# Moving the inverse of block 2 behind the weight conversion, and block 2's solve five steps later in block 1

## The chip, the cores and the metric

The kernel runs on one core of one Trainium2 chip. The metric is device time in microseconds (us). PE is the matmul engine, PEld its weight loads, DVE the vector engine, ACT the scalar engine, SP the engine whose queue issues most DMAs.

## The reference

A delta-rule attention for 4 sequences of 8 heads, 768 time steps of width 48, followed by a two-layer network:

```python
k_n = k / (np.linalg.norm(k, axis=-1, keepdims=True) + 1e-06)
for t in range(S):                       # state: one 48 x 48 matrix per head
    y[:, :, t] = q_t @ state
    state = state + beta_t * outer(k_t, v_t - state^T k_t)
x = y.transpose(0, 2, 1, 3).reshape(B * S, H * D)    # 3072 x 384
h = x @ w_in                                          # 384 x 2048
out = np.maximum(0.01 * h, h) @ w_out                 # 2048 x 384
```

All in float32; each network matmul is done as three matmuls over split operands (a high part and a remainder).

## The kernel before

The 768 steps are cut into 12 blocks of 64. For block n there are these pieces, each a Python generator that is advanced one step at a time:

- `gram(n)`: two steps (groups). It loads k and q, forms the products of the keys with keys and queries on PE (`pg`, L201), copies them (L205), masks the query part on DVE (`rq`, L216; `gm`, L220), and sends the key part through DRAM (`gd`) into the tile `L`.
- `inv(b)`: 33 steps, blocks 0 and 1 together as b = 0, then block n as b = n - 1, so block 2 is b = 1. It clears the tile `T` (L280), calls `norms` (twelve short DVE instructions, L239 to L248), scales `L` (L289, L292), and then makes 31 elimination steps, each of up to two products (`tmp`, L263) and two subtractions (L268) on DVE. At the end ACT makes a transposed copy (L299) and SP writes both to DRAM (`td`, `tt`; L307, L308). `T` has one buffer, so the next inverse's clearing waits until those transfers have read it.
- `solve(n)`: five steps. It loads the inverse back (`rt`, `gm`; L318, L320) and goes through matmuls and copies `pz`, `zs`, `pu`, `rt`, `pk`, `pw`, `pc`, `py`, `ys`. It needs the inverse of block n and the state of block n - 1. A DVE step in it, `rv` (L388), scales keys and values by the norms.
- `ffn(n)`: the network on the 256 rows of block n, in 16 steps over f; step f makes nine matmuls `ph` (L468), two ACT instructions (`gh`, L472, L473), one DVE remainder (`gl`, L475), and six matmuls `po` (L458) two steps later; `gh` and `gl` have three buffers each. A seventeenth step first calls `columns(n + 1)`, which turns `ys` of the next block into the split operands `xh`, `xl` (`px` L443, L115, L116), and then writes the output. `ffn(n + 1)` can't start without those.
- `weights()`: 32 chunks, each some seven DVE instructions (L148 to L161) and two ACT ones, which unpack the network's weights from 64-bit words. Four are converted early, 28 run into block 0. `ffn(0)` step f needs chunks 2f and 2f + 1.

The function `weave(n_slots, (generator, steps, a, b), ...)` traces one step of each slot in turn and spreads `steps` of a generator evenly over the slots a to b. In block n there are 17 slots: `ffn(n)` in all, the weights in 0 to 12 of block 0, `solve(n + 1)` in 2 to 11, `inv` (of block n + 2) in 2 to 17, `gram` in 11 to 13. A generator that needs another (`need`) advances it first.

The order of the trace is only a priority. The framework puts the instructions in order per engine by a simulated timeline: of those that are ready, the one traced first goes. On the chip each engine then works through its list in that fixed order. `behind(name)` adds an order on one engine: what it encloses is put behind a marked instruction. In `norms`, the first DVE instruction is put behind the last `gl` traced so far.

Of the kernel before, what the change touches and what calls it, by code (L numbers as in the profile page):

```python
# [14 lines left out]
ALU = mybir.AluOpType  # L15
# [10 lines left out]
NGR = NSEQ // GS  # L26
# [21 lines left out]
def delta_moe_kernel(ctx: ExitStack, tc, kqT, kv, qT, beta, cst, w_all, out, nblk):  # L48
# [10 lines left out]
    nc = tc.nc  # L59
    NFC, _, DO = w_all.shape[1:]  # L60
# [47 lines left out]
    raws, mark = {}, {}  # L108

    def behind(name):  # L110

        return tc.issue_after(mark[name]) if name in mark else nullcontext()
# [5 lines left out]
    def load_w(k, gate=None):  # L118
        if k < 2 * NFC:
            raws[k] = raw = sb.tile([P, DO], U64, tag=f"w{k}", name=f"wr{k}", bufs=1)  # L120
            if gate:
                with behind(gate):
                    nc.vector.memset(raw[:, 0:1].bitcast(F32), 0.0)
            with behind("L"):
                nc.sync.dma_start(raw, w_all[:, k // 2, k % 2])

    def weights():

        for k in range(2 * NFC):
            f, x = k // 2, k % 2
            words = raws.pop(k).bitcast(F32).rearrange("p (n two) -> p two n", two=2)
            lo, hi = words[:, 0], words[:, 1]
            loi, hii = lo.bitcast(U32), hi.bitcast(U32)
            g = sb.tile([P, DO], F32, tag="cg", name=f"cg{k}", bufs=CB)
            r = sb.tile([P, DO], F32, tag="cr", name=f"cr{k}", bufs=1)
            gi, ri = g.bitcast(U32), r.bitcast(U32)

            def final():  # L140
                t = sb.tile([P, 2 * DO], F32R, tag=f"w{k}", name=f"w{k}", bufs=1)
                for e in range(2):
                    (wi, wo)[x][e][f] = t[:, e * DO:(e + 1) * DO]
                return (w[f] for w in (wi, wo)[x])

            nc.scalar.activation(g, hi, AF.Abs)
            with behind("inverse" if k >= KA else None):
                i = nc.vector.tensor_scalar(g, g, HI_MIN, HI_MAX, ALU.max, ALU.min)  # L148
            mark["work"] = i.ins
            if k + WAHEAD >= WEARLY:  # L150
                load_w(k + WAHEAD, "work")

            e = sb.tile([P, DO], F32, tag="ce", name=f"ce{k}", bufs=1)
            nc.vector.tensor_scalar(gi, gi, 3, 0x3FFFF000, ALU.logical_shift_left, ALU.bitwise_and)
            nc.vector.scalar_tensor_tensor(gi, hii, 0xC0000000, gi, ALU.bitwise_and, ALU.bitwise_or)  # L155
            nc.vector.tensor_scalar(ri, hii, 0x1FF, 14, ALU.bitwise_and, ALU.logical_shift_left)
            nc.vector.scalar_tensor_tensor(ri, loi, 18, ri, ALU.logical_shift_right, ALU.bitwise_or)  # L157
            nc.vector.tensor_scalar(e.bitcast(U32), gi, 0xFF800000, None, ALU.bitwise_and)
            d0, d1 = final()
            nc.scalar.copy(d0, g)  # L160
            nc.vector.scalar_tensor_tensor(d1, ri, 2.0 ** -34, e, ALU.mult, ALU.mult)  # L161
            yield

    Lh, gm, nrm, Tts, ys, xs, done = {}, {}, {}, {}, {}, {}, set()
# [5 lines left out]
    def dq(n):  # L170

        return nc.scalar if n < 2 else nc.sync
# [58 lines left out]
    def norms(n, n2):  # L231

        p, w = P, HC
        s, r, c, z = (sb.tile([P, wd], F32, tag=t, name=f"{t}{n}", bufs=b)
                      for t, wd, b in (("sr", HC, 1), ("rc", HC, 1), ("cb", HC, 2), ("sq", C, 2)))
        nrm[n] = z
        dq(2 * n).dma_start(c, beta[n])
        with behind("gl"):
            nc.vector.tensor_scalar(s.bitcast(U32), n2.bitcast(U32), 1, None, ALU.logical_shift_right)  # L239
        nc.vector.tensor_scalar(s, s, SQRT_SCALE, 1e-30, ALU.mult, ALU.max)  # L240
        for f in (NEWTON, 0.5):
            nc.vector.reciprocal(r, s)
            nc.vector.scalar_tensor_tensor(r, r, f, n2, ALU.mult, ALU.mult)
            nc.vector.scalar_tensor_tensor(s, s, f, r, ALU.mult, ALU.add)
        nc.vector.tensor_scalar_add(s, s, EPS)
        nc.vector.reciprocal(r, s)
        nc.vector.tensor_tensor(c, c, r, ALU.mult)
        nc.vector.tensor_tensor(c, c, r, ALU.mult)  # L248
        for e in range(2):
            nc.scalar.mul(z[:, e * HC:(e + 1) * HC], s, half[:, e:e + 1])  # L250
        return c
# [20 lines left out]
    def inv(b):  # L272
# [8 lines left out]
        yield  # L281
        L = Lh.pop(b)
        c = norms(b, L.rearrange("p m i -> p (m i)")[:, ::HC + 1])
        if two:
            nc.vector.tensor_copy(X[:, ::HC + 1], c)
# [208 lines left out]
    def chain(fn, blocks):  # L494
        for n in blocks:
            yield from fn(n)

    def weave(n_slots, *streams):

        taken = [0] * len(streams)  # L500
        for i in range(n_slots):
            for k, (gen, steps, a, b) in enumerate(streams):
                want = steps if i >= b - 1 else max(0, i + 1 - a) * steps // (b - a)
                while taken[k] < want:
                    next(gen, None)
                    taken[k] += 1

    NS, NF, NI = NSLOT, NFC + 1, HC + 1
    wg = weights()
    gg = chain(gram, range(nblk))  # L510
    iv = chain(inv, range(len(NB)))
    sv = chain(solve, range(nblk))
    ff = chain(ffn, range(nblk))
# [10 lines left out]
        load_w(k)  # L524
    for n in range(nblk):

        weave(NF, (ff, NF, 0, NF), (wg, 2 * NFC * (n == 0), 0, 12), (sv, NS * (n + 1 < nblk), 2, 11),
              (iv, NI * (n + 2 < nblk), 2, NF), (gg, NGR * (n + 3 < nblk), 11, 13))


WAHEAD, WEARLY = 8, 14
# [66 lines left out]
```

## Time and profile before

| | us |
|---|---|
| three runs, median | 724.42 |
| three runs, lowest and highest | 723.74, 728.68 |
| profiled execution, device time | 727.48 |
| profiled execution, span of its instructions | 725.7 |

| engine | busy us | share of the span |
|---|---|---|
| PE | 627.9 | 87% |
| PEld | 581.4 | 80% |
| DVE | 499.6 | 69% |
| ACT | 323.8 | 45% |

The busy share is a mean over stages. The span has a start without the network (to about 92 us), block 0 with the conversion of the weights (to about 174 us), and eleven further blocks.

### The profile page before, as it was taken

How to read it: one execution, taken by the hardware profiler on the slowest of the kernel's cores; microseconds unless marked ns; L12 is line 12 of the kernel's file. 1: busy time of each engine (PE TensorE's matmuls, PEld its weight loads, DVE VectorE, ACT ScalarE, POOL GpSimd, SP SyncE). 2: the span in 40 equal slices, each digit the busy share in tenths (PEclk: the TensorE clock that was granted, in tenths of full speed). 3: DMA queues.
4: the chain of work that ended last, by engine and by line, in shares of the span. 5: the costliest groups of instructions: out<-in, count | busy, mean ns of one | idle time of the engine just before them, and what ended most of it. 6: DMA issues, size and time to landing. Idle time of an engine off the chain costs nothing.

```text
span 725.7 us, 20966 instructions
## 1 busy us (share of the span) xinstructions
PE 627.9 (87%) x8296; PEld 581.4 (80%) x8296; DVE 499.6 (69%) x2222; ACT 323.8 (45%) x830; POOL 7.4 (1%) x12
## 2 busy tenths in 40 slices
PE   5200789948997999999999999999999999999996
PEld 4100679838986998998989989989989989999996
DVE  7798999999594765866955956947858659532221
ACT  3112656624444463553454444534634635544432
POOL 4000000000000000000000000000000000000000
PEclk9999999967998999999999999999999999999999
DMA  8495783610306427036045064073171260310000
GB/s 196 94 308 106 196 213 91 162 37 23 46 2 121 102 46 162 17 68 153 3 90 131 4 117 105 7 139 77 30 146 48 46 132 2 63 29 2 1 22 23
DMA packets 130786, 60.91 MB, mean 84 GB/s; under 512 B 115392, under 2 KB 118592, under 8 KB 130688
## 3 DMA queue, kind: packets, MB, share of 16 engines
q1 hardware_dynamic: 117376, 56.81, 34.9%
q10 hardware_dynamic: 13312, 2.76, 2.1%
q8 instruction: 65, 1.06, 0.6%
q14 instruction: 33, 0.27, 0.1%
HBM read 46.96 MB, written 12.58 MB: 82 GB/s over the span
## 4 chain that ended last, share of the span: by engine, by line
PE 61%; DVE 22%; DMA 7%; ACT 4%; issue 3%; SPq 2%; ACTq 1%; DVEq 0%
PE ph L468 25%; PE po L458 22%; DMA tt<-T 3%; PE pk L383 3%; DVE rq L216 3%; PE pw L396 3%; DVE rv L388 3%; DVE T L268 2%; DVE tmp L263 2%; PE pu L342 2%; PE pz L334 2%; SPq L307 2%; DVE cg L155 1%; DVE w L161 1%; DVE cr L157 1%
## 5 line engine op out<-in xcount | busy, mean ns | idle before, releaser
L468 PE MATMUL ph<-xh,w 128*128 128x256 f32 x1152 | 257.3, 296 | 10.0 <-DVE gl L475 6.9
L468 PEld LDWEIGHTS ph<-xh,w 128*128 128x128 f32 x1152 | 195.9, 193 | 21.5 <-DVE gl L475 9.7
L458 PE MATMUL po<-w,gh 128*128 128x384 f32 x768 | 192.0, 347 | 8.7 <-ACT w L160 4.9
L475 DVE TENSOR_TENSOR gl<-ph,gh 128x256 fp32r<-128x256 f32 x192 | 80.6, 423 | 134.4 <-ACT ph L473 123.6
L468 PE MATMUL ph<-xl,w 128*128 128x256 f32 x576 | 166.0, 289 | 1.9 <-DVE xl L116 1.1
L472 ACT ACTIVATE gh<-ph 128x256 fp32r<-128x256 f32 x192 | 73.5, 383 | 173.2 <-PE ph L468 170.8
L458 PEld LDWEIGHTS po<-w,gh 128*128 128x128 f32 x768 | 134.1, 193 | 12.1 <-ACT w L160 5.6
L458 PE MATMUL po<-w,gl 128*128 128x384 f32 x384 | 119.7, 345 | 0.0
L468 PEld LDWEIGHTS ph<-xl,w 128*128 128x128 f32 x576 | 111.3, 193 | 4.3 <-DVE xl L116 4.0
L268 DVE TENSOR_TENSOR T<-T,tmp 128x60 f32<-128x60 f32 (+35 forms) x661 | 112.3, 207 | 1.3
L263 DVE TENSOR_TENSOR tmp<-T,L 128x60 f32<-128x60 f32 (+35 forms) x661 | 112.4, 208 | 0.7
L473 ACT ACTIVATE ph<-ph 128x256 f32<-128x256 f32 x192 | 73.1, 381 | 0.0
L458 PEld LDWEIGHTS po<-w,gl 128*128 128x128 f32 x384 | 68.9, 193 | 0.5
L334 PE MATMUL pz<-rt,gm 32*32 32x32 f32 x768 | 19.9, 197 | 34.8 <-DMA rt<-td 34.8
L201 PE MATMUL pg<-kq 48*64 48x128 f32 x768 | 38.5, 301 | 12.5 <-DMA kq<-in_kqT 7.2
L334 PEld LDWEIGHTS pz<-rt,gm 32*32 32x32 f32 x768 | 16.0, 111 | 37.7 <-DMA rt<-td 35.2
L201 PEld LDWEIGHTS pg<-kq 48*64 48x64 f32 x768 | 30.6, 147 | 19.4 <-DMA kq<-in_kqT 8.0
L216 DVE TENSOR_TENSOR rq<-pg,csb 64x256 f32<-64x256 f32 x96 | 40.6, 423 | 1.7
L280 DVE MEMSET T<- 128x512 f32 (+1 forms) x11 | 5.8, 524 | 39.7 <-DMA tt<-T 30.2
L385 ACT ACTIVATE rt<-pk 48x512 f32<-48x512 f32 x44 | 26.1, 593 | 12.6 <-PE pk L383 11.9
L160 ACT CAST w<-cg 128x384 fp32r<-128x384 f32 x32 | 16.1, 510 | 33.6 <-DVE cr L157 24.5
L398 ACT COPY rv<-pw 64x384 f32<-64x384 f32 x48 | 22.7, 472 | 16.1 <-PE pw L396 15.2
(61 smaller groups left out, 651.4 us busy)
## 6 DMA issues: line engine op xcount, KB each, us to landing
wr<-in_w_all SPq DMA_DIRECT2D x32, 384.0 KB, 5.3
kq<-in_kqT SPq DMA_DIRECT2D x44, 192.0 KB, 3.7
L<-gd SPq DMA_DIRECT2D x22, 256.0 KB, 3.9
rk<-in_kv SPq DMA_DIRECT2D x24, 192.0 KB, 3.4
rv<-in_kv SPq DMA_DIRECT2D x24, 192.0 KB, 4.1
rq<-in_qT SPq DMA_DIRECT2D x24, 192.0 KB, 3.8
out<-ob SPq DMA_DIRECT2D x48, 96.0 KB, 2.7
gd<-gs SPq DMA_DIRECT2D x88, 32.0 KB, 2.8
```

Source lines behind the costliest of these rows:

```text
L201: nc.tensor.matmul(ps[b][c * 64:(c + 1) * 64, p * 128:(p + 1) * 128], kq[r, c ^ b, p, 0], kq[r, c ^ b, p].rearrange("p x t -> p (x t)"), s ...
L216: nc.vector.tensor_tensor(qa[DN, c, b * NPAIR:(b + 1) * NPAIR], pv[b][r, 1], tri[r].rearrange("p (o t) -> p o t", o=1).broadcast_to([C, NP ...
L263: nc.vector.tensor_tensor(tv, t[:, :, j:j + 1].broadcast_to([P, k, w]), L[:, j, j + 1:].rearrange("p (o w) -> p o w", o=1).broadcast_to([P ...
L268: i = nc.vector.tensor_tensor(t, t, tv, ALU.subtract)
L334: nc.tensor.matmul(zv[h * 64:h * 64 + HC, u], gt[lo, l], t[lo, h, u, HC:], start=True, stop=True)
L385: nc.scalar.mul(t[UP, c], pv[c * 64:c * 64 + D], -1.0)
L398: nc.scalar.copy(v[DN, c], pv[c * 64:c * 64 + C])
L458: i = nc.tensor.matmul(po[t][:, :DO], a[:, ts_], w[f], start=(f == 0 and k == 0), stop=(f == NFC - 1 and k == 2))
L468: nc.tensor.matmul(ph, a[f][:, cc * P:(cc + 1) * P], x[cc][e], start=(k == 0), stop=(k == 3 * NCC - 1))
L472: nc.scalar.activation(gh, ph, AF.Prelu, alpha=0.01)
L473: i = nc.scalar.activation(ph, ph, AF.Prelu, alpha=0.01)
L475: i = nc.vector.tensor_tensor(gl, ph, gh.bitcast(F32), ALU.subtract)
```

## The change

The last DVE instruction of each weight chunk is marked. In `norms` for block 2 (n == 1 there) the first DVE instruction is put behind that mark, so behind the last chunk's last instruction, and no longer behind a `gl`. The steps of that inverse are traced in slots 12 to 17 of block 0 and no longer in 2 to 17. `gram(2)`, which it used to pull forward to slot 2, is traced in slots 11 and 12 instead; of `gram(3)` one group follows in slot 12 and one at slot 2 of block 1. In block 1, `solve(2)` is traced in slots 7 to 16 (was 2 to 11) and `gram(4)` in slot 16 (was 11 to 13). From block 2 on the trace is as before.

```diff
-            nc.vector.scalar_tensor_tensor(d1, ri, 2.0 ** -34, e, ALU.mult, ALU.mult)
+            i = nc.vector.scalar_tensor_tensor(d1, ri, 2.0 ** -34, e, ALU.mult, ALU.mult)
+            mark["weights"] = i.ins
             yield
...
-        with behind("gl"):
+        with behind("weights" if n == 1 else "gl"):
             nc.vector.tensor_scalar(s.bitcast(U32), n2.bitcast(U32), 1, None, ALU.logical_shift_right)
...
-        weave(NF, (ff, NF, 0, NF), (wg, 2 * NFC * (n == 0), 0, 12), (sv, NS * (n + 1 < nblk), 2, 11),
-              (iv, NI * (n + 2 < nblk), 2, NF), (gg, NGR * (n + 3 < nblk), 11, 13))
+        d = 5 if n == 1 else 0
+        weave(NF, (ff, NF, 0, NF), (wg, 2 * NFC * (n == 0), 0, 12), (sv, NS * (n + 1 < nblk), 2 + d, 11 + d),
+              (iv, NI * (n + 2 < nblk), 2 if n else 12, NF), (gg, NGR * (n + 3 < nblk), 11 + d, min(13 + d, NF)))
```

## Rows read from the trace of the kernel before

**Rows 1.** The page's second part: DVE's busy share in tenths, in 40 slices of 18.1 us.

```profile
DVE  7798999999594765866955956947858659532221
```

**Rows 2.** Busy time by stretch of the span: for each engine the us busy and, in brackets, the instructions; PEclk is the granted clock.

```profile
111.80:172.80 61.00, 48.58 (x575) 43.01 (x574) 59.91 (x218) 31.60 (x77) 0.00 (x0) 0.83 0.32 79
172.80:233.40 60.60, 54.76 (x712) 50.10 (x711) 42.54 (x235) 27.12 (x69) 0.00 (x0) 0.96 0.29 49
...
286.90:337.60 50.70, 50.13 (x702) 46.43 (x702) 35.90 (x177) 24.76 (x66) 0.00 (x0) 1.00 0.37 80
```

**Rows 3.** DVE in order of time: the last instruction of two early weight chunks and of the last one (start us, duration us); and the output copy of `ffn(0)` on ACT.

```profile
84.80 0.55 DVE L161 SCALAR_TENSOR_TENSOR w<-cr,ce 128x384 fp32r<-128x384 uint32 x1
...
87.29 0.55 DVE L161 SCALAR_TENSOR_TENSOR w<-cr,ce 128x384 fp32r<-128x384 uint32 x1
...
172.25 0.55 DVE L161 SCALAR_TENSOR_TENSOR w<-cr,ce 128x384 fp32r<-128x384 uint32 x1
...
174.56 0.86 ACT L487 COPY ob<-po 128x384 f32<-128x384 f32 x2
```

**Rows 4.** Groups of DVE instructions from 111.8 to 172.3 us: count, busy us and mean ns, and the idle time before them with what ended it.

```profile
L268 DVE TENSOR_TENSOR T<-T,tmp 128x60 f32<-128x60 f32 (+21 forms) x32 | 5.6, 204 | 0.1
L263 DVE TENSOR_TENSOR tmp<-T,L 128x60 f32<-128x60 f32 (+21 forms) x32 | 5.5, 205 | 0.0
...
L216 DVE TENSOR_TENSOR rq<-pg,csb 64x256 f32<-64x256 f32 x8 | 3.4, 423 | 0.2
L388 DVE TENSOR_TENSOR rv<-rv,nt 64x384 f32<-64x384 f32 x4 | 2.0, 555 | 0.0
...
L239 DVE TENSOR_SCALAR sr<-L 128x32 uint32<-128x32 uint32 x1 | 0.2, 192 | 1.1 <-DMA L<-gd 1.1
```

**Rows 5.** DVE in order of time: the first and the last of the twelve `norms` instructions of the first inverse, which ran alone; the scaling of `L` for block 2; two neighbouring pairs of its elimination.

```profile
33.55 0.19 DVE L239 TENSOR_SCALAR sr<-L 128x32 uint32<-128x32 uint32 x1 [4.17 <-DMA L<-gd]
...
36.54 0.19 DVE L248 TENSOR_TENSOR cb<-cb,rc 128x32 f32<-128x32 f32 x1
...
126.94 0.36 DVE L289 COPY T<-cb 64x16 f32<-64x16 f32 x2
127.32 1.30 DVE L292 TENSOR_TENSOR L<-L,cb 128x512 f32<-128x512 f32 x2
...
173.66 0.36 DVE L268 TENSOR_TENSOR T<-T,tmp 128x75 f32<-128x75 f32 x2
173.95 0.35 DVE L263 TENSOR_TENSOR tmp<-T,L 128x70 f32<-128x70 f32 x2
```

**Rows 6.** SP's queue in order of time: four weight loads that wait for DVE; and, from the chain of waits, the transfer of `gram(3)`'s `L`.

```profile
113.11 15.87 SPq L125 DMA_DIRECT2D wr<-in_w_all  x4
...
147.28 3.39 DMA L<-gd
```

**Rows 7.** DVE in order of time: two `gl` of `ffn(1)` amid block 2's elimination, the end of that elimination, the clearing of `T` for block 3, the end of block 3's elimination, and what follows on DVE up to the start of `ffn(2)`.

```profile
180.13 0.41 DVE L475 TENSOR_TENSOR gl<-ph,gh 128x256 fp32r<-128x256 f32 x1
...
182.22 0.42 DVE L475 TENSOR_TENSOR gl<-ph,gh 128x256 fp32r<-128x256 f32 x1
...
185.68 0.17 DVE L268 TENSOR_TENSOR T<-T,tmp 128x8 f32<-128x8 f32 x1
...
193.66 0.48 DVE L280 MEMSET T<- 128x512 f32 x1 [2.55 <-DMA tt<-T]
...
216.80 0.17 DVE L268 TENSOR_TENSOR T<-T,tmp 128x8 f32<-128x8 f32 x1
225.17 0.48 DVE L280 MEMSET T<- 128x512 f32 x1 [8.20 <-ACT ob L487]
225.67 1.75 DVE L216 TENSOR_TENSOR rq<-pg,csb 64x256 f32<-64x256 f32 x4
...
230.44 0.42 DVE L116 TENSOR_TENSOR xl<-px,xh 128x256 fp32r<-128x256 f32 x1
...
232.90 0.76 DVE L116 TENSOR_TENSOR xl<-px,xh 128x256 fp32r<-128x256 f32 x2
```

**Rows 8.** Block 2's solve in block 1: its first matmuls on PE, its last copy on ACT, the `ph` of `ffn(2)` that had waited for the last `xl`; then PE's work between 195.9 and 219.8 us, as a stretch and as two groups of it.

```profile
195.94 0.69 PE L334 MATMUL pz<-rt,gm 32*32 32x32 f32 x32 [1.41 <-DMA rt<-td]
...
221.04 0.48 ACT L416 COPY ys<-py 128x384 f32<-128x384 f32 x1
...
233.38 0.58 PE L468 MATMUL ph<-xl,w 128*128 128x256 f32 x1 [0.49 <-DVE xl L116]
...
195.90:219.80 23.90, 23.86 (x459) 21.77 (x459) 18.70 (x122) 13.14 (x30) 0.00 (x0) 0.93 0.08 14
...
L468 PE MATMUL ph<-xh,w 128*128 128x256 f32 x30 | 6.7, 296 | 0.0
L458 PE MATMUL po<-w,gh 128*128 128x384 f32 x20 | 6.2, 410 | 0.0
```

**Rows 9.** The solve of block 0, before any network work (its first `pz`, and the first `ph` of `ffn(0)`); and, from the chain of waits, the landing of block 4's inverse in DRAM and the first `pz` of block 4.

```profile
70.30 1.06 PE L334 MATMUL pz<-rt,gm 32*32 32x32 f32 x32 [33.37 <-DMA rt<-td]
...
91.73 0.64 PE L468 MATMUL ph<-xh,w 128*128 128x256 f32 x2
...
269.99 3.83 DMA tt<-T
...
293.26 0.62 PE pz L334 x32
```

## The prediction, made before the changed kernel was run

> **What bounds the kernel now.** I read the slices first, then the stretches, then DVE's order of time, last the chain of waits. The slices [rows 1] show DVE at nine tenths or more from about 72 us to 180 us and half busy afterwards. The stretches [rows 2] make that exact. From 111.8 us to the end of the last weight chunk at 172.8 us DVE is busy 59.9 of 61.0 us, while PE has 48.6 us of work, part of it at the lower clock (granted 0.83). So the end of block 0 is set by DVE: the conversion of the weights, with everything that stands among it. From about 287 us on it is PE: 50.1 of 50.7 us, and nothing that the change touches happens there. Block 1 lies between: 60.6 us where a later block takes 50.7. The change is worth what it does to one instant, the start of `ffn(2)`, now 233.4 us [rows 8]; what comes after is moved along with it, if the later inverses still arrive in time.
>
> **What leaves the weight stretch.** The conversion alone takes 2.49 us a chunk (84.80 to 87.29) [rows 3]; block 2's inverse is what slows it from 111.8 us on. Its parts there, as time by which the next DVE instruction starts later: the wait for `L` in front of L239, 1.1 us [rows 4]; the twelve norms instructions, 3.2 us when alone (33.55 to 36.73) [rows 5], less where other work fills the gaps between dependent ones, so an estimated 2.6 us; the scaling, 0.4 + 1.3 us [rows 5]; 64 elimination instructions [rows 4], which by their pairs (173.66 to 173.95 for two) take 0.13 us each, 8.3 us, and not the 0.20 us of their durations, since the next one starts before the last has ended [rows 5]; and block 2's four `rv`, 2.0 us, which need the norms [rows 4]. Sum: 1.1 + 2.6 + 1.7 + 8.3 + 2.0 = 15.7 us. `gram(3)`'s DVE work (eight `rq`, 3.4 us [rows 4], and its copies) may leave as well, but `gram(2)`, now traced late, should take its place; I count nothing, with 0 to 4 us as bounds. So the last chunk should end near 172.8 - 15.7 = 157 us (153 to 158). `ffn(0)` ends 1.8 us behind it today (172.8 to 174.56) [rows 3], so near 159 us. PE's 48.6 busy us in the stretch include matmuls at half speed; it can keep up, with little to spare, and that is why I take the upper part of the bounds.
>
> **What is moved past which queue.** `gram(2)` loses its early place. Its matmuls, copies, and ten transfers on SP (eight into `gd`, two into `L`) should run about where `gram(3)` runs now, whose `L` landed at 147.28 + 3.39 = 150.7 us [rows 6]. SP's list has weight loads in front that wait for DVE (15.9 us for four) [rows 6]; these are issued by 129 us, so `L` is there before 157 us and costs nothing. If it were late, the inverse would wait, not the weights. The beta load and the inverse's own writes keep their order on SP.
>
> **What it costs behind.** The inverse is the same DVE work in another order. DVE has done, by 185.85 us, all weights and all of block 2's inverse [rows 7], with almost no idle time. After the change it must do the same by then. Added: `ffn(1)` is some 15 us or seven steps further, so seven `gl`, at a step of 0.34 us each, 2.4 us. Saved: the 1.1 us wait. I put the end of block 2's inverse at 187 us (184 to 192), about where it is. From there to the first `pz` it took 195.94 - 185.85 = 10.1 us (transposed copy, write to DRAM, read back) [rows 7, 8]; unchanged, so `pz` at 197 us. The gain then comes from what PE has left to do at that moment. Today it has five steps of `ffn(1)` mixed into the solve (30 `ph` at six a step, 20 `po` at four) [rows 8], each 2.1 us by the spacing of `gl` (180.13 to 182.22) [rows 7]: 10.5 us. After the change `ffn(1)` starts near 159 us and its 16 steps, 34 us, are done by about 193 us. So the solve has PE to itself.
>
> **The solve alone.** Today `pz` to the end of `ys` is 195.94 to 221.52, 25.6 us; less 10.5 us is 15.1 us. From `ys` to `ffn(2)` it is 11.9 us today, and this is a queue: the clearing of `T` for block 4 stands on DVE in front of `rq` of `gram(4)` and of `xl`, and it was held until the transfers of block 3's inverse had landed (8.2 us idle; the named releaser is not what it needs) [rows 7]. Without it and without the `rq` (225.67 to 230.44, 4.8 us) I leave 5 us. 15 + 5 = 20 us. The other bound is block 0's solve, on a PE that had idled: 70.30 to 91.73, 21.4 us, without the stage `pk` [rows 9], so up to 26 us with an estimated 2 to 5 us for that. I take 22 us: `ffn(2)` at 197 + 22 = 219 us (213 to 225).
>
> **Sum.** 233.4 - 219 = 14.4 us. The profiled execution's 727.48 us becomes 713.1 us; it lies 3.06 us above the median of the runs, so the median goes from 724.42 to 710.0 us. Later blocks can be early by this much: block 4's `pz` stood at 293.26 us, 19.4 us behind the landing of its inverse (269.99 + 3.83) [rows 9], and block 3's inverse, which starts 8 us behind block 2's (185.85 to 193.66) [rows 7] and keeps its instant, is ready at about 228 us, early in `ffn(2)`.
>
> **A rule against the change.** PE's idle time is collected into one gap in front of `ffn(2)`. The row of block 0's first `pz`, behind 33 us of idleness, has 1.06 us for 32 matmuls; the same 32 in block 2, behind a gap of 1.41 us, took 0.69 us [rows 8, 9]. The Trainium skill (TensorE: Matmul & The Clock Gate, section "Why this matters for your kernels") advises against idle gaps in the middle of a kernel, since PE then falls back to half its clock; by it the change pays in the chain what it saves in the queue. The two rows agree that a long gap costs a clock level. Its price is the upper end of the solve, 26 us, plus some 2 us for the first steps of `ffn(2)`: `ffn(2)` at 225 us, a gain of 8 us, the time 716 us. It is inside the forecast's own range.
>
> **Rivals.** (a) The solve stays mixed with `ffn(1)`. If the planned order puts steps of `ffn(1)` behind `pz`, and PE waits there, those 10.5 us come back: `ffn(2)` at 225 to 231 us, the time 716 to 722 us, say 719. For it: `solve(2)` is traced late. Against: PE has ready work of lower priority which a planner fills in. (b) The clearing of `T` keeps its place in front of `xl`. Block 3's inverse ends when it does now, so `ffn(2)` starts at 231 to 236 us: 722 to 727 us, no change. For it: that is the order today. Against: `xl` would be ready some 10 us before the clearing. The same time results if the change does not do what it says, the conversion being no faster. (c) Slower: the inverse starves `ffn(1)`. Its steps are all traced in block 0 and so all come before every `gl` of `ffn(1)`. If DVE's list is filled by the inverse from 157 to 187 us, PE stops after the three steps that the buffers allow; then 13 steps (27 us), the solve's own PE work (about 13 us, the 23.9 us stretch less 10.5) and 5 us for `xl` remain, with part at the lower clock: 187 + 45 + 4 to 8, `ffn(2)` at 236 to 240 us, the time 727 to 731 us, say 729. It decides from the point where more than about eight `gl` stand behind the inverse. Against: the tail of this inverse has the same priority over `gl` today, and `gl` came every 2.1 us in it [rows 7], since dependent instructions leave gaps.
>
> **How the numbers follow.** Forecast 0.56 (704 to 716 us), (a) 0.22, (b) 0.12, (c) 0.10. About 1%, 7.2 us, is what a measurement of this kernel can tell from no change. Faster by more: the forecast and a little of (a), 0.60. Within: most of (a), (b), a fifth of (c), 0.32. Slower: 0.08. The range runs from 703 us, where `gram` work leaves the stretch too, to 725 us, which leaves out (c) and some of (b).
>
> **What would show it.** The last L161 near 157 us, with no L263 before it; the end of block 2's elimination between 184 and 192 us; `pz` of block 2 near 197 us, and PE idle in front of it; `xl` of block 2 ahead of block 4's clearing of `T`; `ph` of `ffn(2)` near 219 us; blocks of 51 us from there. Wrong if the eliminations end much later than 192 us, or if a transfer or a clearing stands in a list in front of `gl` or `xl`.

## The result and the profile after

The changed kernel takes 732.14 us (median; 729.96 to 735.27), the kernel before, on the same chips, 726.62 us: a ratio of 1.0079, 95% interval 1.0064 to 1.0094. It is 5.5 us slower; forecast were 710.0 us and a range of 703 to 725. (The forecast started from 724.42 us, the median of three runs of the kernel before; the 726.62 us are the median of 20.) The profiled execution has a span of 729.7 us, 4.0 us more than before.

The stretches of [rows 2] after the change:

```profile
111.80:172.80 61.00, 55.59 (x661) 49.12 (x660) 57.02 (x177) 32.85 (x86) 0.00 (x0) 0.94 0.42 100
172.80:233.40 60.60, 48.61 (x610) 44.86 (x609) 41.55 (x261) 22.03 (x53) 0.00 (x0) 0.77 0.26 46
...
286.90:337.60 50.70, 49.41 (x699) 45.72 (x698) 35.87 (x176) 24.51 (x65) 0.00 (x0) 1.00 0.35 72
```

Until 172.8 us PE does 7.0 us more work than before, at a granted clock of 0.94 in place of 0.83. Then the lead is lost: up to 233.4 us PE does 6.2 us less, at 0.77 in place of 0.96.

DVE in order of time, for [rows 3] and [rows 7]: the last weight, the first of block 2's norms, four `gl` of `ffn(1)`, the end of block 2's inverse, two clearings of `T`, two groups of `xl`, then `gl` of `ffn(2)` (the first, fourth and eighth) and block 4's norms.

```profile
156.04 0.56 DVE L161 SCALAR_TENSOR_TENSOR w<-cr,ce 128x384 fp32r<-128x384 uint32 x1
156.52 0.18 DVE L240 TENSOR_SCALAR sr<-L 128x32 uint32<-128x32 uint32 x1
...
164.46 0.42 DVE L476 TENSOR_TENSOR gl<-ph,gh 128x256 fp32r<-128x256 f32 x1 [1.33 <-ACT ph L474]
...
186.03 0.42 DVE L476 TENSOR_TENSOR gl<-ph,gh 128x256 fp32r<-128x256 f32 x1 [0.18 <-ACT ph L474]
...
188.14 0.42 DVE L476 TENSOR_TENSOR gl<-ph,gh 128x256 fp32r<-128x256 f32 x1 [0.27 <-ACT ph L474]
...
194.48 0.42 DVE L476 TENSOR_TENSOR gl<-ph,gh 128x256 fp32r<-128x256 f32 x1 [0.31 <-ACT ph L474]
194.82 0.16 DVE L269 TENSOR_TENSOR T<-T,tmp 128x8 f32<-128x8 f32 x1
...
200.78 0.48 DVE L281 MEMSET T<- 128x512 f32 x1 [5.80 <-DMA tt<-T]
...
228.23 0.48 DVE L281 MEMSET T<- 128x512 f32 x1 [7.46 <-DMA tt<-T]
...
229.61 0.42 DVE L116 TENSOR_TENSOR xl<-px,xh 128x256 fp32r<-128x256 f32 x1
...
232.83 0.76 DVE L116 TENSOR_TENSOR xl<-px,xh 128x256 fp32r<-128x256 f32 x2 [1.28 <-ACT xh L115]
...
239.22 0.42 DVE L476 TENSOR_TENSOR gl<-ph,gh 128x256 fp32r<-128x256 f32 x1 [0.82 <-ACT ph L474]
...
245.96 0.19 DVE L240 TENSOR_SCALAR sr<-L 128x32 uint32<-128x32 uint32 x1 [3.00 <-DMA L<-gd]
...
247.53 0.36 DVE L476 TENSOR_TENSOR gl<-ph,gh 128x256 fp32r<-128x256 f32 x1
...
258.67 0.42 DVE L476 TENSOR_TENSOR gl<-ph,gh 128x256 fp32r<-128x256 f32 x1
```

The last weight starts 16.2 us earlier, the inverse ends 9.1 us later than in [rows 7], and the eighth `gl` of `ffn(2)` comes at 258.67 us. The same in the kernel before: the first `gl` (with the second), block 4's norms, the fourth and the eighth `gl`.

```profile
236.25 1.00 DVE L475 TENSOR_TENSOR gl<-ph,gh 128x256 fp32r<-128x256 f32 x2 [2.59 <-ACT ph L473]
...
240.35 0.18 DVE L239 TENSOR_SCALAR sr<-L 128x32 uint32<-128x32 uint32 x1
...
242.14 0.43 DVE L475 TENSOR_TENSOR gl<-ph,gh 128x256 fp32r<-128x256 f32 x1
...
253.63 0.42 DVE L475 TENSOR_TENSOR gl<-ph,gh 128x256 fp32r<-128x256 f32 x1
```

So the eighth `gl` is 5.0 us late; behind it the distance stays between 3.8 and 5.0 us to the end. The whole loss lies before it. Two views tell where the way there got longer. PE after, for [rows 8]: block 2's `pz`, a stage of its solve, two groups of `gram(4)`'s matmuls, the first `ph` on an `xl`, a further group, and the `ph` on the last `xl` of the first step.

```profile
202.08 1.07 PE L335 MATMUL pz<-rt,gm 32*32 32x32 f32 x32 [5.90 <-DMA rt<-td]
...
214.73 3.54 PE L397 MATMUL pw<-rv,rt 128*64 128x48 f32 x61
...
224.31 1.09 PE L202 MATMUL pg<-kq 48*64 48x128 f32 x16
...
226.09 1.97 PE L202 MATMUL pg<-kq 48*64 48x128 f32 x16
...
233.36 0.58 PE L469 MATMUL ph<-xl,w 128*128 128x256 f32 x1
...
234.51 1.97 PE L202 MATMUL pg<-kq 48*64 48x128 f32 x16
...
237.01 0.41 PE L469 MATMUL ph<-xl,w 128*128 128x256 f32 x1
```

In the kernel before the 64 `pg` ran in one piece, ahead of `ffn(2)`, and its first `ph` on an `xl` followed:

```profile
219.80 2.87 PE L201 MATMUL pg<-kq 48*64 48x128 f32 x64
...
231.39 0.36 PE L468 MATMUL ph<-xl,w 128*128 128x256 f32 x1
```

The `ph` of [rows 8] that had waited for the last `xl` (233.38 us) is the third of that step on an `xl`; its place is now 237.01 us, 3.6 us later, though the last `xl` is written when it was (233.59 us for 233.66). In front of it stand 16 `pg`.

ACT after: the output copy of `ffn(1)`, and the last `ys`.

```profile
196.04 0.86 ACT L488 COPY ob<-po 128x384 f32<-128x384 f32 x2
...
224.28 0.48 ACT L417 COPY ys<-py 128x384 f32<-128x384 f32 x1
```

And the SP queue's issue of `gram(4)`'s `L`, first after, then before:

```profile
241.25 1.10 SPq L225 DMA_DIRECT2D L<-gd  x2
```

```profile
233.94 1.10 SPq L224 DMA_DIRECT2D L<-gd  x2
```

### The profile page after: what moved, and what is told of

Same layout as the page of the kernel before. It is cut to its first block, busy times and chain, and to the rows that moved or that the text cites. A ratio compares the mean times of both kernels' runs of the same rounds, so it can differ in the third digit from the quotient of the medians.

```text
span 729.7 us, 20959 instructions
## 1 busy us (share of the span) xinstructions
PE 632.1 (87%) x8296; PEld 585.5 (80%) x8296; DVE 500.8 (69%) x2222; ACT 323.2 (44%) x830; POOL 7.3 (1%) x12
## 4 chain that ended last, share of the span: by engine, by line
PE 56%; DVE 23%; DMA 8%; ACT 5%; issue 3%; SPq 3%; ACTq 1%; DVEq 0%
PE ph L469 24%; PE po L459 21%; DVE T L269 3%; DMA tt<-T 3%; DVE tmp L264 3%; DVE rq L217 3%; PE pk L384 2%; DVE rv L389 2%; PE pw L397 2%; PE pu L343 2%; SPq L308 2%; PE px L444 2%; PE pz L335 1%; DVE gl L476 1%; DVE cg L155 1%
## 5 line engine op out<-in xcount | busy, mean ns | idle before, releaser
L459 PE MATMUL po<-w,gh 128*128 128x384 f32 x768 | 187.0, 342 | 2.3 <-ACT gh L473 2.3
L459 PEld LDWEIGHTS po<-w,gh 128*128 128x128 f32 x768 | 132.3, 190 | 4.6 <-ACT gh L473 4.2
L459 PE MATMUL po<-w,gl 128*128 128x384 f32 x384 | 117.4, 341 | 0.0
L202 PE MATMUL pg<-kq 48*64 48x128 f32 x768 | 43.1, 311 | 15.3 <-DMA kq<-in_kqT 6.9
L202 PEld LDWEIGHTS pg<-kq 48*64 48x64 f32 x768 | 33.7, 153 | 23.5 <-issue 10.3
L206 ACT COPY gs<-pg 128x256 f32<-128x256 f32 x48 | 16.0, 373 | 34.7 <-PE pg L202 34.7
```

Of the source, the lines that this page charges most:

```text
L202: nc.tensor.matmul(ps[b][c * 64:(c + 1) * 64, p * 128:(p + 1) * 128], kq[r, c ^ b, p, 0], kq[r, c ^ b, p].rearrange("p x t -> p (x t)"), s ...
L459: i = nc.tensor.matmul(po[t][:, :DO], a[:, ts_], w[f], start=(f == 0 and k == 0), stop=(f == NFC - 1 and k == 2))
```

## The experiments

Theories at the start: A, a longer serial chain (the inverse alone on DVE, then the solve on a slow PE, then `gram(4)` in front of `ffn(2)`); B, the later trace of `solve(2)` and `gram(4)`; C, the clearing of `T` in front of `xl`. All ratios are to the kernel before on the same chip; medians of different runs can come from different chips, so two runs are compared by their ratios.

**Parts of the change.** Only the trace order, with the norms behind a `gl` as before:

```diff
-        with behind("weights" if n == 1 else "gl"):
+        with behind("gl"):
```

> The changed kernel, but the norms of block 2 stay behind a gl and not behind the last weight; the trace order is the changed one. Theory A (the loss is a serial chain: block 2's inverse, alone on DVE, ends 9 us later than before, 195.0 against 185.9 us, and the solve behind it runs on a PE at its lower clock): the norms start once L has landed, near 150 us, so some of the inverse goes back among the last weights; last weight at 158 to 162 us, inverse done at 190 to 194 us, the time 2 to 4 us below the changed kernel's. Theory B (the loss is the later trace of solve(2) and gram(4) in block 1): that is still in, so the same time as the changed kernel within 1 us.

Measured: 727.52 us, ratio 1.0026 (1.0006 to 1.0045). The last weight now starts at 160.3 us, the inverse ends at 192.4 us, and the wait of block 4's norms for `L` is 1.75 us in place of 3.00. Against B; most of the loss comes with the edge behind the weights (0.0026 above the kernel before are left of 0.0079).

Without the later trace in block 1:

```diff
-        d = 5 if n == 1 else 0
+        d = 0
```

> The changed kernel with solve(2) and gram(4) traced in block 1 where they were before (slots 2 to 11 and 11 to 13). Theory A: the solve cannot start before its inverse, so its first pz stays near 202 us; only the 64 pg of gram(4) may leave the start of ffn(2), some 3 us: 1 to 3 us below the changed kernel, still slower than before. Theory B: the loss goes, the time is that of before or less.

Measured: 733.74 us, 1.0115 (1.0077 to 1.0152). B falls. Block 4's norms start even later, at 247.4 us: tracing `gram(4)` earlier doesn't bring its `L` sooner.

**A second buffer for `T`**, in the changed kernel and in the kernel before:

```diff
-        X = sb.tile([P, HC * HC], F32, tag="T", name=f"T{b}", bufs=1)
+        X = sb.tile([P, HC * HC], F32, tag="T", name=f"T{b}", bufs=2)
```

> The changed kernel with two buffers for T. The clearing of T for blocks 3 and 4 then waits for no transfer: the 5.8 us and 7.5 us of DVE idleness in front of them go, block 3's inverse ends near 215 us. Theory A: the solve of block 2 is a chain of its own and stays (pz near 202 us, ys near 225 us); the xl behind it come up to 3 us earlier: 2 to 4 us below the changed kernel. Theory C (the clearing in front of xl is the whole loss): 5 us or more below it, level with before.

> The kernel before with two buffers for T, to price the clearing's wait (8.2 us of DVE idleness ahead of ffn(2)) without the change. If the wait is what sets the start of ffn(2) there (233.4 us), it starts at 226 to 229 us and the time falls by 4 to 7 us. If the output rows and px set it, less than 2 us.

Measured: 727.11 us, 1.0033 (1.0006 to 1.0059), and 725.59 us, 1.0003 (0.9977 to 1.0029). By the ratios the changed kernel gains 3.3 us, as A said, and not the 5 or more of C. Its first `ph` on an `xl` came at 230.0 us in place of 233.4, but then DVE stood 6.12 us at block 4's norms, waiting for `L` until 243.3 us, with a `gl` behind it. The kernel before fits neither of its expectations: its first `gl` of `ffn(2)` came 7.4 us earlier (228.89 for 236.25), but the norms then waited 7.72 us, the eighth `gl` came at 252.83 us (253.63), and the time stayed. This was the hint to theory F: the norms of block 4 stand in DVE's list in front of a `gl` of `ffn(2)`, and their `L` lands late.

**The clock.** Extra matmuls in PE's idle time:

```diff
             columns(n + 1)
+        if n == 1:
+            for _ in range(130):
+                nc.tensor.matmul(hbank[1][:, 1], wi[0][0][:, 0:P], wi[0][0][:, 0:TB], start=True, stop=True)
```

> The changed kernel with 130 extra matmuls (128x128 by 256, results thrown away) traced behind block 2's columns in block 1, so that PE fills its idle time between ffn(1) and ffn(2) and its granted clock stays up; nothing else is altered. Theory A (a longer serial chain: inverse, solve, clearing of T): the solve's PE work gets faster, pz (202 us) to the end of ys falls from 22.7 us to 16-19 us, but block 3's inverse still ends near 220 us on DVE and the clearing of T for block 4 still stands in front of xl near 228 us, so ffn(2) gains only on its first steps: 729-731.5 us against 732.1. Theory D (the lower clock alone makes the loss): xl and ffn(2) come 5-6 us earlier, 726 us or less.

Measured: 731.39 us, 1.0087 (1.0054 to 1.0120), the clock at 1.00 (190 to 210 us) and 0.97 (210 to 233.4 us). `pz` to the end of `ys` took 21.5 us (204.7 to 226.2) against 22.7, where A had said 16 to 19, and the clearing now waited 10.8 us. D falls. It isn't a clean price, since the extra matmuls also stand in front of others.

**`gram(2)` early again:**

```diff
         d = 5 if n == 1 else 0
+        if n == 0:
+            need(gg, gram, 2)
```

> The changed kernel with gram(2) traced early in block 0 again, as in the kernel before (and gram(3) with it in the old place); the inverse still stands behind the last weight. Theory A: some 4.7 us of rq and gm instructions leave the stretch between the last weight and the inverse's end, the last weight ends 1-4 us later (157-160 us), block 2's inverse ends at 190-193 us instead of 195, and the time is 727-731 us. Rival G (the inverse is paced by the gl of ffn(1) alone, every 2.1 us): the inverse still ends at 194-196 us and the time is 731-734 us.

Measured: 729.69 us, 1.0054 (1.0038 to 1.0070). The time is where A put it, the mechanism isn't: the last weight starts at 160.2 us, and the inverse ends at 194.9 us as without the edit, which is what G said (its time, 731 to 734 us, was missed). What came earlier is block 4's `L` (244.3 us).

**Block 4's norms later** (slots 6 to 17), and the same with two buffers for `T`:

```diff
-              (iv, NI * (n + 2 < nblk), 2 if n else 12, NF),
+              (iv, NI * (n + 2 < nblk), {0: 12, 2: 6}.get(n, 2), NF),
```

> The changed kernel with block 4's inverse traced in slots 6 to 17 of block 2 and no longer in 2 to 17, so that its norms stand behind a later gl; nothing else is altered. Theory F: gram(4), traced five slots later, lands L late, and block 4's norms wait for it on DVE in front of a gl of ffn(2) (3.0 us idle at 246 us; none in the kernel before). Then the fourth gl of ffn(2) comes at 244-245 us instead of 247.5 and the time is 728-730 us. Theory A without F (that wait is covered, ffn(2) is set by PE's lower clock and gram's matmuls): the fourth gl stays at 247 us, 731-733 us.

> The changed kernel with two buffers for T and block 4's inverse traced in slots 6 to 17 of block 2. Theory A with F: with two buffers ffn(2) could start at 228 us, but block 4's norms then wait 6.1 us for L (at 243.3 us) in front of a gl; with that wait gone too, the fourth gl comes at 239-241 us instead of 244.5, the later blocks are 3.5-5 us ahead of the run with two buffers alone, and the time is 721.5-724 us, 2-4 us under the kernel before. Rival H (another wait of ffn(2), solve(3) or a later inverse, takes its place): 726-728 us, as with two buffers alone.

Measured: 733.76 us, 1.0112 (1.0085 to 1.0139), and 725.05 us, 0.9996 (0.9978 to 1.0014). The fourth `gl` came at 245.9 us (F had said 244 to 245), and at 235.9 us with two buffers (239 to 241); the times lie outside of every range expected. Both lost it one block further on, where the inverse that was now late held the clearing for block 5, and this stands in front of `gl` and `xl`. DVE in the first of the two:

```profile
291.17 0.48 DVE L281 MEMSET T<- 128x512 f32 x1 [6.22 <-DMA tt<-T]
291.57 0.36 DVE L476 TENSOR_TENSOR gl<-ph,gh 128x256 fp32r<-128x256 f32 x1
...
293.97 0.76 DVE L116 TENSOR_TENSOR xl<-px,xh 128x256 fp32r<-128x256 f32 x2
```

**The clearing put behind `gl`**, in the changed kernel and in the kernel before:

```diff
-        nc.vector.memset(T, 0.0)
+        with behind("gl"):
+            nc.vector.memset(T, 0.0)
```

> The changed kernel with the clearing of T put behind the last gl traced so far, as the norms are, so that it can't stand in front of xl; T keeps its one buffer. Theory C' (the clearing's wait of 7.5 us in front of xl holds up ffn(2), one part of the loss): xl and the first ph of ffn(2) come 3-6 us earlier (227-230 us instead of 233.4), part of it is lost again at block 4's norms, which wait for L at 243 us, and the time is 726.5-729.5 us against 732.1. Rival (xl waits for the solve and for gram(4)'s matmuls anyway): 731-733 us.

> The kernel before with the clearing of T put behind the last gl traced so far, for comparison: it removes the 8.2 us of DVE idleness in front of rq and xl near 225 us. If that wait holds up ffn(2) in the kernel before, too: 721-724 us against 725.6. If xl is bound by the solve and PE there: 724.5-726.5 us.

Measured: 726.33 us, 1.0007 (0.9985 to 1.0030), and 723.27 us, 0.9951 (0.9924 to 0.9978). As a time C' is met, as a place it isn't: up to the eighth `gl` of `ffn(2)` (260.28 us) nothing is gained on the changed kernel's 258.67; the gain of 5.8 us in the span comes in the later blocks, and the kernel before has it too. The clearing ahead of `xl` explains little of the difference between the two: 0.0056 of the 0.0079 are left. In the kernel before, block 4's norms now wait as well: DVE reaches them sooner (238.39 us for 240.35), and `L` is issued later (238.59 us for 233.94):

```profile
244.08 0.19 DVE L239 TENSOR_SCALAR sr<-L 128x32 uint32<-128x32 uint32 x1 [5.69 <-DMA L<-gd]
...
256.71 0.42 DVE L476 TENSOR_TENSOR gl<-ph,gh 128x256 fp32r<-128x256 f32 x1
```

**Pacing.** The `gl` of `ffn(1)` step f behind elimination step 3(f + 1) of block 2's inverse:

```diff
+        if b == 1:
+            mark[f"e{j}"] = i.ins
...
+            with behind(f"e{min(HC - 2, 3 * (f + 1))}" if n == 1 else None):
                 i = nc.vector.tensor_tensor(gl, ph, gh.bitcast(F32), ALU.subtract)
```

> The changed kernel with the gl of step f of ffn(1) put behind elimination step 3(f + 1) of block 2's inverse (the last ones behind its end), so that DVE's list has three elimination steps for each gl and not two; nothing else is altered. Theory P (the inverse ends late because DVE, in its fixed order, waits for PE at each gl, and so ends with the last gl of ffn(1)): block 2's inverse ends at 184-189 us instead of 195.0, ffn(1) still ends by 200 us, pz comes at 191-196 us, the rest follows, and the time is 722-727 us. Rival S (the eliminations are a serial chain that takes that long whatever the list): the inverse ends at 192 us or later, and the time is 730 us or more.

Measured: 727.49 us, 1.0013 (0.9990 to 1.0036). From the start of the norms (158.65 us) the inverse takes 34.4 us, in the changed kernel 38.5. P is half right: 1.8 us less are idle (3.05 for 4.89), and the other 2.2 us are five `gl` that now stand behind its end. Its instant of 184 to 189 us was missed, as the inverse ended at 193.0 us, again right behind a `gl` that had kept DVE idle (1.38 us). S has that instant right and the time wrong.

Pacing, clearing behind `gl`, and block 4's inverse from slot 4 on:

> The changed kernel with three things together: the clearing of T behind gl, the gl of ffn(1) paced as three elimination steps to one, and block 4's inverse traced in slots 4 to 17 of block 2, so that its norms stand behind a later gl. Theories C', P and F together: the inverse ends at 184-189 us, pz at 191-196 us, ffn(2)'s first ph at 215-221 us, no wait of DVE over 2 us in front of the first gl of ffn(2): 714-721 us. If the solve at the lower clock is what remains: 721-725 us. If the late inverse of block 4 is missed later on: 725 us or more.

Measured: 720.36 us, 0.9925 (0.9893 to 0.9957). The time is in the range expected, the instants aren't: the inverse ended at 193.3 us and the first `ph` on an `xl` came at 227.9 us. Slot 4 was too early: DVE still waited 7.51 us for `L`, until 247.1 us.

**Clearing behind `gl` and block 4's inverse from slot 7 on**: the changed kernel, the same with pacing, the kernel before, and the changed kernel with two buffers for `T` besides:

> The changed kernel with the clearing of T behind gl and block 4's inverse traced in slots 7 to 17 of block 2, so that the norms stand behind a gl at about 249 us, when L has landed (247 us in the run with slot 4). Theory F: the wait for L of gram(4) in front of gl is what is left of the loss once the clearing is out of the way; without it the first eight gl of ffn(2) are done at 253-255 us instead of 260.3, and the time is 720.5-723.5 us, 2.5-5 us below the run with the clearing alone (726.3). Rival E (the later inverse of block 4 is missed by solve(4), and the gain goes there): 725-728 us.

> As the run with clearing and late inverse in slots 7 to 17, and with the gl of ffn(1) paced as three elimination steps to one. Theories P and F: a wait of 7.5 us for L in front of a gl, which the run with pace, clearing and slot 4 still had at 247 us, is gone: the first eight gl of ffn(2) are done at 249-252 us, the time is 714-718 us against 720.4. Rival E: 719-722 us.

> For comparison, the kernel before with the same two edits that lie outside the change: the clearing of T behind gl, and block 4's inverse in slots 7 to 17 of block 2. In the kernel before the norms of block 4 hardly waited for L, so nothing is gained over the clearing alone: 722.5-725 us. If the change of the order is worth something by itself once its own new waits are gone, the run with pace, clearing and late inverse is at least 4 us below this one; if not, within 2 us of it.

> As the run with clearing and late inverse in slots 7 to 17, with two buffers for T besides. If a free T lets block 3's inverse and what follows run earlier: block 3's inverse ends at 213-217 us instead of 222, its reads on SP and gram(4)'s writes behind them come 5 us earlier, the time is 717-720.5 us. If the second buffer gives nothing any more once the clearing stands behind gl: within 1.5 us of that run.

Measured: 719.05 us, 0.9904 (0.9869 to 0.9939); 719.35 us, 0.9890 (0.9861 to 0.9918); 718.97 us, 0.9882 (0.9855 to 0.9908); 716.50 us, 0.9853 (0.9827 to 0.9880). F is shown in the kernel before, which had been expected to gain nothing: against the clearing alone its first `gl` of `ffn(2)` stays (234.81 us for 234.88), the wait of 5.69 us is gone, the eighth `gl` comes 6.0 us earlier, and the ratio falls by 0.0069, 5.0 us. In the changed kernel the ratio falls by 0.0103, 7.5 us, but F isn't the whole of it: the eighth `gl` comes 9.5 us earlier (250.75 for 260.28), and the first already 6.5 us (234.78 for 241.32), ahead of the norms. From the last weight up to there the two traces have the same order of instructions on PE, DVE and ACT, but for a few missing records. From the end of `ys` to the first `gl`, the clearing alone, then both edits:

```profile
227.07:241.32 14.25, 14.25 (x86) 11.53 (x82) 5.72 (x15) 3.17 (x9) 0.00 (x0) 0.50 0.85 168
```

```profile
226.41:234.78 8.37, 8.37 (x89) 6.83 (x86) 5.72 (x15) 3.19 (x10) 0.00 (x0) 1.00 0.71 138
```

The granted clock is the lower level, 0.50, in the one and the higher one in the other: PE is busy throughout in both, and the difference is 5.9 us in the same order of work. Why it rose in the one and not in the other isn't shown. Block 4's norms in the changed kernel, then the eighth `gl` in the kernel before, both with these two edits:

```profile
251.63 0.12 DVE L240 TENSOR_SCALAR sr<-L 128x32 uint32<-128x32 uint32 x1
```

```profile
250.68 0.42 DVE L476 TENSOR_TENSOR gl<-ph,gh 128x256 fp32r<-128x256 f32 x1 [0.30 <-ACT ph L474]
```

No wait for `L` is left, and the eighth `gl` come at 250.75 and 250.68 us. The difference of 3.6 us that the clearing alone had left there is gone, in the trace and in the time; it was 6.4 us at the first `gl`, which are level now too, and so this pair doesn't tell the late `L` from the clock. With pacing the time lies in the range of rival E (719 to 722 us), not in that of P and F: it gains nothing here. The second buffer did not do what was expected of it: block 3's inverse ended at 221 us, not at 213 to 217, and the eighth `gl` at 250.53 us is where it was. Its lower time is not in this trace: the profiled execution took 719.13 us at a granted clock of 0.967 over its span, the other five 715.74 to 716.72 us at 0.973 to 0.976.

**The best version's edits on the kernel before**, and pacing, clearing and slot 7 with 100 extra matmuls:

> For comparison, the kernel before with all three edits that lie outside the change: two buffers for T, the clearing of T behind gl, block 4's inverse in slots 7 to 17 of block 2. The changed kernel with the same three took 716.5 us. If the order of block 2's inverse is worth nothing once the waits around ffn(2) are gone, this run is within 2 us of that; if the change gains there, it is at 719 us or more; if the change still costs something, below 714.5 us.

> The changed kernel with clearing behind gl, late inverse of block 4 and pacing, and with 100 extra matmuls (128x128 by 256, results thrown away) traced behind block 2's columns, which fill PE's gaps in the solve. Without them the solve went from pz at 199.4 us to ys at 221 us, with PE at a granted clock of 0.65 from 210 to 233 us, and the gl of ffn(2) began at 234.7 us, as in the kernel before with the same edits, though ys was ready 4 us earlier. Theory D' (PE at its lower level takes those 4 us back): the clock is over 0.9 in that stretch, the first gl of ffn(2) comes at 229-231.5 us, the time is 714-717 us. Rival (the solve and the start of ffn(2) are bound by copies, DMAs and DVE): the first gl stays at 233.5-236 us, 718.5-722 us.

Measured: 721.66 us, 0.9931 (0.9901 to 0.9962), and 720.66 us, 0.9923 (0.9895 to 0.9950). With all three edits the changed order is ahead by 0.0078, some 5.7 us, which the expectation (719 us or more) had named as a gain of the change; with two of them it is level, and the second buffer moves the ratio by -0.0051 in one order and +0.0049 in the other. So the change gains beside one set of edits and not beside another; that it gains by itself isn't shown. The extra matmuls are told below.

## Why the prediction was wrong

**Right: what leaves the weight stretch.** -15.7 us was said, -16.2 us came (172.25 to 156.04 us). (One term of the sum was misread: 0.29 us for two eliminations is 0.145 each, 9.3 us for 64 and not 8.3.) `ffn(0)` was copied out from 161.7 us, 2.7 us later than said; `ffn(1)` was copied out from 196.04 us ("by about 193"). `pz` had PE idle in front of it, 5.90 us.

**Wrong: "the inverse is the same DVE work in another order", so 187 us.** It ended at 194.98 us. DVE's busy time up to the inverse's end, before and after:

```profile
111.80:185.85 74.05, 72.40 (x295) 0.86 0.29 71
```

```profile
111.80:195.00 83.20, 76.71 (x299) 0.96 0.31 73
```

Of the 9.15 us more, 4.3 are busy and 4.8 idle (6.49 against 1.65). The count of instructions is nearly the same. Two terms of the step were wrong. First, "with almost no idle time" was a property of the order before. Weights stood ready between the dependent instructions; with them gone DVE, in its fixed list, waits at each `gl` for PE. What DVE waited for in the same two stretches, before and after (total us, times, longest):

```profile
DVE gl L475 <- ACT ph L473: 0.4, 2, 0.2
```

```profile
DVE gl L476 <- ACT ph L474: 4.6, 12, 1.3
```

The spacing 186.03 to 188.14 is PE's step of 2.11 us, with not quite three elimination steps in it, and the inverse ends right behind the last `gl`. From the start of the norms to that end PE is busy 36.2 of 38.5 us: what sets the end is PE's way through `ffn(1)`, which the prediction itself had let run until 193 us, and not the sum of DVE's work. Second, `gram` was counted at nothing, with a gain as one bound: in fact eight `rq` more (3.4 us) and four `gm` (1.2 us) lie in this time, since `gram(2)` joined `gram(3)` and didn't take its place, and nine more `gl` (3.1 us at the step of 0.34), not seven; against that stand two weight chunks fewer (5 us at 2.49 [rows 3]). That is 2.7 of the 4.3 us; the rest isn't counted out. This term didn't move the end: with `gram(2)` early again the inverse started 4.2 us later, took 34.2 us with PE busy in all of them, and ended at 194.9 us as before.

**Wrong: "the solve alone", 15.1 us.** `pz` to the end of `ys` took 22.7 us (202.08 to 224.76) against 25.6. I had subtracted all 10.5 us of `ffn(1)`; 2.9 came. Those steps had run mostly in the solve's own gaps: it is a chain of copies, transfers and DVE steps, among block 3's inverse. The two kernels with clearing and slot 7 show this without other differences in front: pacing, on the changed order, `pz` at 199.39 us and the end of `ys` at 220.94; on the order before, with `ffn(1)` mixed in, 199.16 and 224.79. So 3 to 4 us were won there, and not 10.5.

**Wrong: "ys to `ffn(2)`, 5 us".** Rival (b) said that the clearing would keep its place in front of `xl`, and it did (228.23 us after a wait of 7.46). I had given it 0.12. From the end of `ys` to the `ph` on the last `xl` it took 12.2 us (224.76 to 237.01), against 11.9 before. But the clearing is not what made it so long: with the clearing out of the way `ys` to the first `gl` took 14.25 us, in the changed kernel 14.46 (224.76 to 239.22). It is PE: its lower clock, and `gram(4)`'s `pg`, whose last groups now stand among the first `ph`. Here the 4 us that the solve had won go. PE from 210.0 to 233.4 us in the two kernels just named, changed order first:

```profile
210.00:233.40 23.40, 22.22 (x309) 19.37 (x310) 13.21 (x76) 9.38 (x20) 0.00 (x0) 0.65 0.48 93
```

```profile
210.00:233.40 23.40, 21.98 (x382) 19.28 (x377) 17.07 (x86) 12.91 (x30) 0.00 (x0) 1.00 0.34 58
```

Granted 0.65 is a mixture of the two levels, 1.2 and 2.4 GHz; 1.00 is the higher one alone. PE is busy as long and does 309 matmuls in place of 382; the 64 `pg` take 7.7 us in five groups, the last from 229.89 us, in place of 2.87 us in one piece. The first `gl` of `ffn(2)` comes 13.7 us behind `ys` in the one, 10.0 us in the other, at 234.65 and 234.81 us: between these two the start of `ffn(2)` hasn't moved.

The rule that the prediction weighed, of the Trainium skill (TensorE: Matmul & The Clock Gate, section "Why this matters for your kernels"), that idle gaps in the middle of a kernel cost PE half its clock, agrees with the trace of the changed kernel: behind the 5.90 us gap `pz` takes 1.07 us (granted 0.50) where it took 0.69 [rows 8] (1.00), and 16 `pg` take 1.97 us at 226.09 (0.50), 1.09 us at 224.31 (1.00). I had put this inside the forecast's range, at 6 us against a gain of 14. What the level costs behind `ys` is the 5.9 us between the two runs above. Extra matmuls didn't win it: with 100 of them the clock stood at 1.00 and the first `gl` still came at 237.0 us, since they take PE's time (23.05 of 23.4 us busy) and stand between the `px`. What the level costs within the solve stays open.

**Missed: `gram(4)`'s way to block 4's norms.** I followed the transfers of `gram(2)` and not those of `gram(4)`. Its matmuls run among those of `ffn(2)` at the lower clock, the last group from 234.51 us, 14.7 us behind the start of all 64 before; its `L` is issued at 241.25 us and not at 233.94; and the norms wait for it on DVE with the fourth `gl` behind them, which turns 3.0 us at the first `gl` (236.25 to 239.22) into 5.4 at the fourth. That wait is absent before, but it isn't the change's alone: where an edit brought `ffn(2)` forward in the kernel before, its norms waited as well (7.72 and 5.69 us), and taking the wait away was worth 6.0 us at the eighth `gl` there. What it alone costs in the changed order isn't shown, since the clock changed with it.

Rival (c), which had the right sign, named another mechanism and was wrong: `ffn(1)` was not starved, its last `gl` came 20.7 us earlier than before (194.48 for 215.2).

**Sum.** The `ph` on the last `xl` was forecast at 219 us, 14.4 us earlier than before, and came at 237.0, 3.6 us later. Of the 18 us between, the inverse has 8 (195.0 for 187), the way from there to `pz` -3 (7.1 us for 10.1), and `pz` to that `ph` 13 (34.9 us for 22). The first `gl` is then 3.0 us late, the fourth 5.4 with the norms in front of it, the eighth 5.0.

## What to carry to other kernels

Work that is "the same in another order" keeps its length only if the new order still has ready instructions between dependent ones: in an engine's fixed list, take away the filler and each instruction that waits for another engine sets the pace. Subtract from a stage only what lay on its path, not all that ran beside it, and for everything that is traced later follow its transfers up to the instruction that waits for them and see what stands behind that one. Before a step is moved, move what stands in front of the late end: two edges on DVE's order (the clearing and the late norms) gave over 1% in either order (in the changed one partly by a higher clock), while the change with these two edges on both sides gave nothing. With a second buffer besides it was ahead, and why isn't shown.

## What was not expected of the hardware

PE at a clock of 1.00 was no faster to the goal than at 0.65, when the clock was held up by work of its own (first `gl` at 237.0 and 234.65 us); where it stood at 1.00 without such work, the same order of instructions took 8.37 us in place of 14.25. And one second buffer for a tile of 4 KB per partition moved the ratio by -0.0046, -0.0051 and +0.0049 in three orders of the same instructions and not at all in a fourth (0.0003); only the first is clear of the intervals, which are 0.003 to 0.007 wide.
